# Float32 tiles for U and the scores in an attention and gated feed-forward kernel

## The chip, the cores and the metric

The kernel runs on one core of a Trainium2 chip. The metric is the time of one execution on the device in microseconds (us), the median of the runs; lower is better. A core has TensorE (matrix products, results in PSUM; its weight loads have a row of their own, PEld), VectorE (DVE), ScalarE (ACT), GpSimd (POOL) and SyncE (SP), which here issues the DMA transfers. Each engine works through its own list of instructions in order.

## The reference

Eight batches, eight heads, 576 tokens, head width 64, 32 memory slots; the model width is 512, the hidden width 1536. The first part compresses each head's keys and values into 32 slots, the second is a gated feed-forward layer on all 4608 tokens:

```
a    = softmax over tokens of phi                  # [b, h, 576, 32]
k_m  = a.T k ;  v_m = a.T v                        # [b, h, 32, 64]
attn = softmax over slots of (q k_m.T / 8)         # [b, h, 576, 32]
x    = attn v_m, heads side by side                # [b * 576, 512]
out  = (sigmoid(x w_gate) * (x w_val)) w_out       # float32
```

Everything but the weights is float32; the three weight matrices arrive as float64.

## The kernel before, in words

The host only rearranges the inputs. The kernel never makes x. It uses x w = attn (v_m w): for a batch and 128 hidden columns (an *f tile*, 12 of them) it makes U = v_m [w_gate | w_val] with one row for each head and slot (8 x 32 = 256 rows, as two groups of 128) and 256 columns, and multiplies the softmax by it. Products that need more than TensorE's fast float32r gives are made as three: each operand is split into a rounded part (`hi`, by ScalarE) and what rounding left (`lo`, a subtraction), and hi hi + lo hi + hi lo are summed in PSUM.

**Memory of a batch** (`memory`): phi's softmax over tokens (`a_max`, `a_exp`), transposed by TensorE (L292, L296), times k and v (L312: float32 products of 32 columns, one for each head of a group, beside one another in TensorE). VectorE scales the result and masks it so that two heads stand block-diagonal; TensorE transposes it (L330).

**Scores and softmax** (`scores`, `s_exp`, `attend`): for each 128 tokens four float32 products, q stationary (128x128) and the block-diagonal k_m moving (64 columns, L367), so tokens lie on the partitions and the softmax over slots is a reduction along the row. Ten transposes by TensorE (L414) then turn the result to [(head, slot), token] in `at_hi` and `at_lo`.

**U** (`make_u`): v_m of two batches (a *pair*) as hi and lo, block-diagonal over both, is the stationary operand; w as hi and lo is moving. For each f tile twelve products of 256 columns (L465 to L467) give U for both batches of the pair. One batch's U is used soon; the other's is parked in SBUF as float32 (`u_par`) and split later (`unpark`). `split_w` splits w anew for every pair: float32 w is kept in DRAM (`w32`), stored once and loaded again for each pair.

**A step** is one batch and one f tile. `gate_half` is called for 256 and for 320 tokens: twelve products (L508), a sigmoid on ScalarE, the multiplication on VectorE (L518), the split of the result (L519, L528). `out_half` multiplies by w_out (L543 to L545) three half steps later (`LAG = 3`). The last 64 tokens of a batch are gathered for `out_left` (L575 to L577).

**Order.** The first pair takes its 24 steps in turns of four f tiles (`CHUNKS`), so that the weights can be converted meanwhile; the other pairs take twelve f tiles of one batch, then twelve of the other. Beside the steps, generators (`sides`) are advanced a piece at a time: the scores, softmax and memory of the batches to come. `convert_w` and `convert_wo` turn float64 words to float32, 512 columns at a time (`to_f32`: one operation on ScalarE, four on VectorE, L132 to L141); `due` spreads them over the first pair. At the very start `queued` fixes the order of the pieces by hand. The scheduler of the framework then places instructions on the engines by its own estimate, so traced order and built order differ. Loads leave SP in the traced order (`load`).

Of the kernel before, what the change touches and what calls it, by code (L numbers as in the profile page):

```python
# [25 lines left out]
CUT = [slice(0, 2 * P), slice(2 * P, S)]   # tokens of one gate / value product  # L26
SCALE = 1.0 / 8.0
# [8 lines left out]
SOLO = 1          # f tiles whose U is made before the second batch's memory is known  # L36
CHUNKS = [4, 4, 4]   # f tiles of the first two batches between their turns
# [3 lines left out]
def attn_moe_kernel(  # L41
    ctx: ExitStack,
    tc: tile.TileContext,
    qT: bass.AP,      # [B, 128 (head of pair, d), 4 * S]   token pieces of (4 pairs, tokens)
    kvm: bass.AP,     # [B, 2, 128, 4, 512]   s = c * 128 + p ; (head, k | v)
    kvt: bass.AP,     # [B, 128, 512]         (group, s - 512)
    phiT: bass.AP,    # [B, 128 (head, m), 2, S]   the second group's last 64 tokens first
    wgv: bass.AP,     # [12, 128, 4, 256]     (gate 128 | value 128), float64 as words
    wo: bass.AP,      # [12, 128, DM]         float64 as words
    out: bass.AP,     # [B * S, DM]  # L50
# [4 lines left out]
    wp = ctx.enter_context(tc.tile_pool(name="wp", bufs=1))  # L55
# [7 lines left out]
    # the accumulators' banks serve too until there is something to accumulate  # L63
# [9 lines left out]
    def att(shape, name, bufs):  # L73
        return sb.tile(shape, F32, name=name, bufs=bufs)
# [3 lines left out]
    # mask[row, j, :] = 1 where the row's head is of parity j  # L78
    mask = keep.tile([P, 2, D], F32, name="mask")
    nc.vector.memset(mask, 0.0)  # L80
    for h in range(4):
        nc.vector.memset(mask[h * M : (h + 1) * M, h % 2, :], 1.0)
# [196 lines left out]
    def memory(b):  # L279
# [55 lines left out]
        if b == 0:  # L335
            nc.scalar.copy(*kmT)
# [561 lines left out]
```

## Time and profile before

| | us |
|---|---|
| runs (3) | 823.63, 824.36, 825.55 |
| median | 824.36 |
| span of the profiled execution | 823.0 |
| TensorE busy in it | 782.0 (95%) |
| VectorE busy | 496.8 (60%) |
| ScalarE busy | 433.1 (53%) |
| GpSimd busy | 195.4 (24%) |

The span runs from the first to the last instruction of one profiled execution. In the views below a row of TensorE's timeline has start, length, line, operation, output <- inputs, tile, shape and count; the ends of products are modelled and overlap, so what one product costs in a stream is read from the distance of two starts, not from its length. A float32 product stands as two records. "L508" is line 508 of the kernel before.

### The profile page before, as it was taken

How to read it: one execution, taken by the hardware profiler on the slowest of the kernel's cores; microseconds unless marked ns; L12 is line 12 of the kernel's file. 1: busy time of each engine (PE TensorE's matmuls, PEld its weight loads, DVE VectorE, ACT ScalarE, POOL GpSimd, SP SyncE). 2: the span in 40 equal slices, each digit the busy share in tenths (PEclk: the TensorE clock that was granted, in tenths of full speed). 3: DMA queues.
4: the chain of work that ended last, by engine and by line, in shares of the span. 5: the costliest groups of instructions: out<-in, count | busy, mean ns of one | idle time of the engine just before them, and what ended most of it. 6: DMA issues, size and time to landing. Idle time of an engine off the chain costs nothing.

```text
span 823.0 us, 13982 instructions
## 1 busy us (share of the span) xinstructions
PE 782.0 (95%) x5394; PEld 699.7 (85%) x5394; DVE 496.8 (60%) x1000; ACT 433.1 (53%) x940; POOL 195.4 (24%) x128
## 2 busy tenths in 40 slices
PE   6887889899899999999999999999999999999997
PEld 5775877788799879998899889999889899999996
DVE  3799997999755564565454464556553654454432
ACT  3557766565534485645325377554424576653222
POOL 1245533435612142311002133220101232310000
PEclk8889999999999999999999999999999999999999
DMA  9857646774732312412030421604000312101001
GB/s 357 327 180 260 246 149 216 256 256 138 241 106 78 134 52 106 167 52 84 30 142 26 160 64 52 219 29 135 1 2 26 104 39 78 53 1 52 1 1 65
DMA packets 30227, 96.33 MB, mean 117 GB/s; under 512 B 3408, under 2 KB 4432, under 8 KB 28112
## 3 DMA queue, kind: packets, MB, share of 16 engines
q1 hardware_dynamic: 30160, 95.43, 33.2%
q8 instruction: 42, 0.69, 0.4%
q14 instruction: 25, 0.20, 0.1%
HBM read 75.50 MB, written 19.92 MB: 116 GB/s over the span
## 4 chain that ended last, share of the span: by engine, by line
PE 73%; DVE 8%; ACT 3%; DMA 3%; issue 2%; SPq 0%; DVEq 0%; ACTq 0%
PE pu_t L508 30%; PE acc L545 9%; PE acc L543 9%; PE acc L544 9%; DMA words<-in_wo_dram 3%; PE pu_t L367 2%; PE pu_t L465 2%; PE pu_t L466 2%; PE pu_t L467 2%; PE pu_t L577 1%; PE pu_t L576 1%; DVE bits L138 1%; PE pu_t L575 1%; DVE g_lo L528 1%; PE pu_t L312 1%
## 5 line engine op out<-in xcount | busy, mean ns | idle before, releaser
L508 PE MATMUL pu_t<-at_hi,u_hi 128*128 128x256 f32 (+1 forms) x768 | 233.5, 304 | 12.4 <-DVE prod L518 6.2
L508 PE MATMUL pu_t<-at_lo,u_hi 128*128 128x256 f32 (+1 forms) x768 | 227.1, 296 | 0.0
L508 PE MATMUL pu_t<-at_hi,u_lo 128*128 128x256 f32 (+1 forms) x768 | 226.6, 296 | 0.2 <-DVE u_lo L116 0.2
L116 POOL TENSOR_TENSOR w_lo<-wraw,w_hi 128x1024 fp32r<-128x1024 f32 (+1 forms) x50 | 117.8, 2356 | 358.1 <-ACT w_hi L204 358.1
L508 PEld LDWEIGHTS pu_t<-at_hi,u_hi 128*128 128x128 f32 x768 | 145.8, 190 | 25.2 <-DVE prod L518 8.6
L518 DVE TENSOR_TENSOR prod<-pu_t,sg 128x256 f32<-128x256 f32 x192 | 87.2, 454 | 128.4 <-ACT sg L103 88.1
L543 PE MATMUL acc<-wo_hi,g_hi 128*128 128x512 f32 x384 | 153.6, 403 | 4.7 <-ACT g_hi L519 2.5
L103 ACT ACTIVATE sg<-pu_t 128x256 f32<-128x256 f32 x192 | 78.4, 410 | 147.0 <-PE pu_t L508 145.8
L544 PE MATMUL acc<-wo_lo,g_hi 128*128 128x512 f32 x384 | 152.0, 396 | 0.0
L508 PEld LDWEIGHTS pu_t<-at_lo,u_hi 128*128 128x128 f32 x768 | 145.8, 190 | 6.5
L545 PE MATMUL acc<-wo_hi,g_lo 128*128 128x512 f32 x384 | 142.9, 399 | 5.3 <-DVE g_lo L528 5.3
L508 PEld LDWEIGHTS pu_t<-at_hi,u_lo 128*128 128x128 f32 x768 | 145.6, 190 | 1.6 <-DVE u_lo L116 0.9
L519 ACT CAST g_hi<-prod 128x256 fp32r<-128x256 f32 x192 | 77.7, 405 | 114.9 <-DVE prod L518 113.3
L528 DVE TENSOR_TENSOR g_lo<-prod,g_hi 128x256 fp32r<-128x256 f32 x168 | 81.6, 486 | 39.0 <-ACT g_hi L519 38.8
L545 PEld LDWEIGHTS acc<-wo_hi,g_lo 128*128 128x128 f32 x384 | 70.9, 189 | 21.2 <-DVE g_lo L528 6.9
L543 PEld LDWEIGHTS acc<-wo_hi,g_hi 128*128 128x128 f32 x384 | 72.5, 189 | 17.5 <-ACT g_hi L519 4.3
L544 PEld LDWEIGHTS acc<-wo_lo,g_hi 128*128 128x128 f32 x384 | 72.6, 189 | 10.2 <-POOL wo_lo L116 0.3
L116 DVE TENSOR_TENSOR u_lo<-pu_t,u_hi 64x512 fp32r<-64x512 f32 x82 | 56.4, 688 | 34.1 <-ACT u_hi L474 32.9
L471 ACT COPY u_par<-pu_t 64x512 f32<-64x512 f32 x110 | 63.4, 579 | 11.1 <-DVE u_lo L116 9.3
L465 PE MATMUL pu_t<-w_hi,vm_hi 128*128 128x256 f32 x196 | 55.2, 286 | 4.1 <-ACT w_hi L204 3.8
L204 ACT CAST w_hi<-wraw 128x1024 fp32r<-128x1024 f32 (+1 forms) x51 | 51.8, 1016 | 13.3 <-DVE wraw L141 13.0
L466 PE MATMUL pu_t<-w_hi,vm_lo 128*128 128x256 f32 x196 | 54.6, 283 | 0.0
(102 smaller groups left out, 1024.1 us busy)
## 6 DMA issues: line engine op xcount, KB each, us to landing
wraw<-w SPq DMA_DIRECT2D x37, 512.0 KB, 3.4
kvm<-in_kvm_dram SPq DMA_DIRECT2D x16, 1024.0 KB, 8.1
words<-in_wgv_dram SPq DMA_DIRECT2D x24, 512.0 KB, 5.2
qt<-in_qT_dram SPq DMA_DIRECT2D x16, 512.0 KB, 6.5
out_dram<-row SPq DMA_DIRECT2D x32, 256.0 KB, 2.4
words<-in_wo_dram SPq DMA_DIRECT2D x12, 512.0 KB, 4.8
w<-wraw SPq DMA_DIRECT2D x12, 512.0 KB, 3.0
ph<-in_phiT_dram SPq DMA_DIRECT2D x8, 576.0 KB, 4.9
```

Source lines behind the costliest of these rows:

```text
L103: last_act[0] = nc.scalar.activation(*args, **kw)
L116: engine.tensor_tensor(lo, x, hi.bitcast(F32), op=ALU.subtract)
L465: nc.tensor.matmul(pb[:, g, :], l_hi, whi[:, kt, :], start=True, stop=False)
L466: nc.tensor.matmul(pb[:, g, :], l_lo, whi[:, kt, :], start=False, stop=False)
L471: nc.scalar.copy(par[j][rs], pb[rs])
L508: nc.tensor.matmul(pt[:, :n], l[:, g, ws], r[:, g, cs], start=(i == 0), stop=(i == 5))
L518: nc.vector.tensor_tensor(prod[:, :n], ps[1][:, :n], sg[:, :n], op=ALU.mult)
L519: nc.scalar.copy(ghi, prod[:, : 2 * P])
L528: nc.vector.tensor_tensor(glo, prod[:, : 2 * P], ghi.bitcast(F32), op=ALU.subtract)
L543: nc.tensor.matmul(o, hi[:, ts], w_hi, start=at_start, stop=False)
L544: nc.tensor.matmul(o, hi[:, ts], w_lo, start=False, stop=False)
L545: nc.tensor.matmul(o, lo[:, ts], w_hi, start=False, stop=at_end)
```

## The change

What it does:

- U is made for one batch at a time. v_m stays float32 and is not split or laid out block-diagonal for two batches: `make_u` multiplies 64x32 of it, one head, by 64 rows of w (which hold that head's part of the model width), for two f tiles at once (512 columns; one f tile for the first four of batch 0). Eight such products, one for each head, fill two PSUM banks. The results are [(head, slot), columns] as before. ScalarE rounds whole banks to `u_hi`, VectorE subtracts for `u_lo`; nothing is parked.
- w_gate | w_val as float32 stays in SBUF for all twelve f tiles (`wg`). Its copy in DRAM, its loads and its splitting are gone.
- The scores are made the other way round: 64x32 of k_m is stationary and q is moving (256 tokens, then 320 as 256 + 64), so heads and slots lie on the partitions. VectorE transposes 32x32 blocks out of PSUM, so that slots lie along the row; after the softmax it transposes back. TensorE's ten transposes for each batch are gone.
- `memory` writes k_m and v_m in float32 without mask.
- In the conversion the limit to float32's range (L132) goes from VectorE to GpSimd.
- Buffers: words 4 (then 2) for 7 (then 3), rows 2 for 3; w_out's first 9 f tiles have room from the start for 8. The table `CONVERT` says at which step each f tile is converted. The first loads leave as phi, k and v, q's first 256 tokens, two pieces of w, the rest of q, the second batch's phi, two pieces of w, the second batch's k and v.
- The remainders of the gates go to GpSimd for batches 0 and 1 (before: batch 0).

The diff, cut:

```diff
-LAG = 3           # half steps between a gate and its product with w_out
-NE = 8            # f tiles of w_out for which there is room from the start
-GAP = 2           # steps from one f tile's U to the next, at least, where there is time
-BITS, ROW, WORDS = 2, 3, (7, 3)   # buffers
+LAG = 3
+NE = 9
+ALONE = 4
+CONVERT = [0, 1, 3, 4, 6, 7, 9, 11, 13, 15, 16]
+WORDS, BITS = (4, 2), (2, 1)
...
+    wg = keep.tile([P, NFT, NKT, 256], F32, name="wg")
...
-    w32 = [dram.tile([P, NKT, 256], F32, name=f"w32_{i}") for i in range(NFT)]
...
+    def to_bits(f, k):
...
         nc.scalar.activation(bits.bitcast(F32), words[:, :, 1].bitcast(F32), AF.Abs)
+        nc.gpsimd.tensor_scalar(
+            bits.bitcast(F32), bits.bitcast(F32), HUGE, TINY, op0=ALU.min, op1=ALU.max
+        )
...
-        nc.vector.tensor_scalar(
-            bits.bitcast(F32), bits.bitcast(F32), TINY, HUGE, op0=ALU.max, op1=ALU.min
-        )
...
+    def of_head(b, w, p):
+
+        rs = slice((p % 2) * D, (p % 2 + 1) * D)
+        hs = slice((p % 4) * M, (p % 4 + 1) * M)
+        return rs, kvTs[b][w][rs, p // 4, hs]
+
+    def scores(b, c):
+
+        n = CUT[c].stop - CUT[c].start
+        nb = n // 32
+        pb = [bank(), bank()]
+        o = 0
+        for u, nu in PIECES[c]:
+            qt = loaded.pop((b, "q", u))
+            for p in range(H):
+                rs, l = of_head(b, 0, p)
+                js = slice((p // 2) * M, (p // 2 + 1) * M)
+                nc.tensor.matmul(
+                    pb[p % 2][js, o : o + nu], l, qt[rs, p // 2, :], start=True, stop=True
+                )
+            o += nu
...
+        for r in range(2):
+            nc.vector.transpose(
+                e[:, r * nb : (r + 1) * nb, :].rearrange("p w m -> p (w m)"), pb[r][:, :n]
+            )
+        mx = att([P, 2 * nb], "mx")
+        nc.vector.tensor_reduce(mx, e, axis=AX.X, op=ALU.max)
+        nc.vector.tensor_tensor(
+            e, e, mx.unsqueeze(2).broadcast_to([P, 2 * nb, M]), op=ALU.subtract
+        )
...
+    def turn(b, c):
...
+        for r in range(2):
+            nc.vector.transpose(
+                t[:, r, :n], e[:, r * n // M : (r + 1) * n // M, :].rearrange("p w m -> p (w m)")
+            )
+        nc.scalar.copy(hi[:, :, cs], t[:, :, :n])
+        rest(lo[:, :, cs], t[:, :, :n], hi[:, :, cs])
...
+    def make_u(b, fs):
+
+        nf = len(fs)
+        pb = [bank()[:, : nf * 256].rearrange("p (f x) -> p f x", f=nf) for _ in range(2)]
+        for p in range(H):
+            rs, l = of_head(b, 1, p)
+            js = slice((p // 2) * M, (p // 2 + 1) * M)
+            r = wg[rs, fs[0] : fs[0] + nf, ORDER[b % 2][p] // 2, :]
+            nc.tensor.matmul(pb[p % 2][js], l, r, start=True, stop=True)
...
+        for r in range(2):
+            nc.scalar.copy(hi[:, r, :nf], pb[r])
+            rest(lo[:, r, :nf], pb[r], hi[:, r, :nf])
...
+    for i, (b, f, at_start, at_end) in enumerate(steps):
...
+        gate_half(b, f, 1)
+        if i + 1 < len(steps) and steps[i + 1][0] != b:
+            run(beside)
+        if i in u_at:
+            make_u(*u_at[i])
...
+        while len(pend) >= LAG:
+            out_half(*pend.pop(0))
```

TensorE's built order in the second or third pair, where a U stands. Before (u, at: U and the softmax; w, vm: w and v_m; pu_t: a PSUM bank):

```order
L508 MATMUL pu_t<-at_hi,u_lo 128x256
L465 MATMUL pu_t<-w_hi,vm_hi 128x256
L466 MATMUL pu_t<-w_hi,vm_lo 128x256
L467 MATMUL pu_t<-w_lo,vm_hi 128x256
L465 MATMUL pu_t<-w_hi,vm_hi 128x256
L466 MATMUL pu_t<-w_hi,vm_lo 128x256
L467 MATMUL pu_t<-w_lo,vm_hi 128x256
```

The same place with the change (wg: the kept w; vT: v_m; acc: the accumulators of the output; L417 to L419 are the products with w_out, L387 those of the gate):

```order
L387 MATMUL pu_t<-at_hi,u_lo 128x320
L356 MATMUL pu_t<-wg,vT 32x512 x4
L417 MATMUL acc_3853<-wo_hi,g_hi 128x512
L418 MATMUL acc_3853<-wo_lo,g_hi 128x512
L419 MATMUL acc_3853<-wo_hi,g_lo 128x512
L417 MATMUL acc_3857<-wo_hi,g_hi 128x512
L418 MATMUL acc_3857<-wo_lo,g_hi 128x512
L356 MATMUL pu_t<-wg,vT 32x512 x4
L419 MATMUL acc_3857<-wo_hi,g_lo 128x512
```

Twelve products in a row have become eight in two runs of four, with products of the output between them; the first run has the four heads with rows 0 to 63, the second those with rows 64 to 127.

VectorE's built order in the third step of the first pair, with the change (sg: the gate's sigmoid and product; bits, words: a piece of float64 weights under conversion; wg and row: its result):

```order
L397 TENSOR_TENSOR sg_616<-pu_t_603,sg_616 128x256
L150 TENSOR_SCALAR bits_493<-bits_493 128x512
L153 SCALAR_TENSOR_TENSOR bits_493<-words_392,bits_493 128x512
L156 SCALAR_TENSOR_TENSOR wg_82<-words_392,bits_493 128x512
L150 TENSOR_SCALAR bits_502<-bits_502 128x512
L153 SCALAR_TENSOR_TENSOR bits_502<-words_400,bits_502 128x512
L156 SCALAR_TENSOR_TENSOR row_501<-words_400,bits_502 128x512
L397 TENSOR_TENSOR sg_657<-pu_t_650,sg_657 128x320
```

Between the two multiplications of one step stand two whole pieces of conversion, three operations each where there were four. Ahead of the first step's multiplication VectorE's order has 2 pieces (before: 3), ahead of the ninth step's 28 (before: 23), ahead of the seventeenth's 36, all of them (before: 32).

More of the change, by code (lines that the diff above doesn't have):

```diff
@@ L271, in a_exp @@
         loaded[b, "rz"] = rz
-    def new_vm(pair):
-        if pair not in vm:
-            vm[pair] = [
-                keep.tile([P, NKT, 2, D], F32R, name=n, bufs=2) for n in ("vm_hi", "vm_lo")
-            ]
     def memory(b):
@@ L477, in unpark @@
-    def unpark(b, f):
-        if (b, f) in U:
-            return
-        par = parked.pop((b, f))
-        hi = mb.tile([P, NG, 256], F32R, name="u_hi", bufs=2)
-        lo = mb.tile([P, NG, 256], F32R, name="u_lo", bufs=2)
-        nc.vector.tensor_copy(hi, par)
-        rest(lo, par, hi, nc.gpsimd if b == 0 else nc.vector)
-        U[b, f] = (hi, lo)
+        kvTs[b] = [keep.tile([P, NG, P], F32, name=f"{w}T", bufs=2 + (w == "v")) for w in "kv"]
+        for w in range(2):
+            nc.scalar.copy(kvTs[b][w], kvT[:, w])
@@ L615, in piece, with step @@
                 next(g, None)
+    def step(do, *args, **kw):
+        with queued():
+            return do(*args, **kw)
     def warm(n):
@@ L648, in attn_moe_kernel @@
[L648 to L659 removed]
+    steps = [s for pair in range(B // 2) for s in turns(pair)]
@@ L660, in attn_moe_kernel @@
+    u_at = {}
+    for i, (b, f, _, _) in enumerate(steps):
+        if b == 0 and f < ALONE:
+            u_at[i - 1] = (b, [f])
+        elif f % 2 == 0:
+            u_at[i - 1] = (b, [f, f + 1])
+    spare = ident.bitcast(mybir.dt.bfloat16)
     idle = po.tile([P, 512], F32, name=f"acc{SF - 1}")
-    once = att([P, NG], "z", 1)[:, :1]
-    with queued():
-        curve(once, mask[:, 0, :1], AF.Exp)
+    once = att([P, NG], "z")[:, :1]
+    step(curve, once, ident[:, :1], AF.Exp)
     load_phi(0)
@@ L681, in attn_moe_kernel @@
-    m0, s0, m1, a0 = memory(0), scores(0), memory(1), attend(0)
-    bits = {}
-    def prepare(f, k):
-        bits[f, k] = to_bits(words_of[f, k])
-    def convert(f, k):
-        both = [None, None]
-        both[k] = bits.pop((f, k))
-        convert_w(f, (k,), both)
-    def step(do, *args, **kw):
-        with queued():
-            do(*args, **kw)
-    def expo(u):
-        s_exp(0, SP_U[u : u + 1])
+    m0, m1 = memory(0), memory(1)
+    bits = {}
     warm(16)
@@ L739, in score @@
     def score(b, then=None):
-        yield from scores(b)
+        for c in range(2):
+            scores(b, c)
+            yield
         if then is not None:
@@ L744, in score @@
             yield
-            yield
-        s_exp(b)
+        for c in range(2):
+            s_exp(b, c)
         if then is not None:
@@ L749, in score, with attend @@
         if b + 1 < B:
-            load_q(b + 1)
+            for c in range(2):
+                load_q(b + 1, c)
         yield
+    def attend(b):
+        for c in range(2):
+            normalize(b, c)
+        yield
+        for c in range(2):
+            turn(b, c)
+            yield
     def remember(b, ready=False):
+        if b >= B:
+            return
         if not ready:
@@ L766, in load_next, with then @@
             load_kv(b)
[L768 to L780 removed]
+    def then(b):
+        return b if b < B else None
+    sides = {0: [m1, score(1), attend(1)]}
```

504 lines of the change are left out of this document (139 added, 365 removed).

## The prediction

> **What bounds the kernel now.** I read the busy times by stretch first. The cuts are the first gate product (38.5 us), the ninth step (129.1), the first step of the second pair of batches (255.7), of the third and fourth pair, the last product of the last gate step (805.8).
>
> ```profile
> core 0: us, PE busy (x) PEld busy (x) DVE busy (x) ACT busy (x) POOL busy (x), PEclk, DMA share, GB/s
> 0.00:38.50 38.50, 29.14 (x306) 24.10 (x306) 22.27 (x55) 16.81 (x35) 6.66 (x15) 0.87 0.91 355
> 38.50:129.10 90.60, 74.75 (x498) 63.73 (x497) 86.71 (x153) 58.58 (x114) 39.94 (x27) 0.92 0.59 211
> 129.10:255.70 126.60, 118.24 (x806) 104.69 (x805) 98.75 (x181) 70.77 (x154) 52.55 (x38) 1.00 0.56 188
> 255.70:445.60 189.90, 188.50 (x1331) 170.80 (x1331) 103.73 (x219) 98.59 (x218) 34.87 (x18) 1.00 0.27 92
> 445.60:635.50 189.90, 188.50 (x1331) 170.79 (x1330) 99.71 (x215) 99.68 (x220) 34.48 (x18) 1.00 0.22 75
> 635.50:805.80 170.30, 170.30 (x1076) 155.65 (x1075) 80.84 (x171) 85.25 (x192) 26.87 (x13) 1.00 0.13 40
> 805.80:823.00 17.20, 12.56 (x55) 9.92 (x53) 4.79 (x10) 3.37 (x8) 0.00 (x0) 0.94 0.23 77
> ```
>
> From 255.7 us to 805.8 TensorE is never idle for long, and VectorE, ScalarE and the DMA engines are half idle: only what TensorE itself has to do counts there. From 38.5 to 129.1 VectorE is busy 86.71 of 90.60 us: it sets the pace. Between 129.1 and 255.7 both are near their limits. The chain of waits gives the price of a step, by the starts of the same products one step apart (start, length, what).
>
> ```profile
> 448.65 1.73 PE pu_t L367 x16
> ...
> 533.46 1.42 PE pu_t L508 x12
> 540.85 1.42 PE pu_t L508 x12
> ...
> 638.55 1.73 PE pu_t L367 x16
> ...
> 790.96 1.76 PE pu_t L508 x12
> 796.89 1.76 PE pu_t L508 x12
> ```
>
> A pair takes 638.55 - 448.65 = 189.90 us. A step that makes a U takes 540.85 - 533.46 = 7.39, one without 796.89 - 790.96 = 5.93, so the twelve products of one U cost 1.46 us of TensorE, whole.
>
> **U, part by part.** Removed are twelve full-array products for each f tile of a pair: 1.46 us. Added are eight float32 products, 64 rows by 32 columns, of 512 columns, for each batch and two f tiles: again one group for each f tile of a pair. The trace has no 64x32 product. The nearest are the 32-column float32 products of the memory (L312), here in TensorE's timeline between full-array products.
>
> ```profile
> 325.40 0.31 PE L508 MATMUL pu_t<-at_lo,u_hi 128*128 128x320 f32 x1
> 325.55 0.31 PE L508 MATMUL pu_t<-at_hi,u_lo 128*128 128x320 f32 x1
> 325.79 1.08 PE L312 MATMUL pu_t<-kvm,e 128*32 128x128 f32 x32
> 326.69 0.40 PE L312 MATMUL pu_t<-kvt,tails 128*32 128x128 f32 x8
> 326.90 1.06 PE L312 MATMUL pu_t<-kvm,e 128*32 128x128 f32 x32
> 327.78 0.40 PE L312 MATMUL pu_t<-kvt,tails 128*32 128x128 f32 x8
> 328.11 0.39 PE L508 MATMUL pu_t<-at_hi,u_hi 128*128 128x256 f32 x1
> 328.33 0.28 PE L508 MATMUL pu_t<-at_lo,u_hi 128*128 128x256 f32 x1
> 328.45 0.28 PE L508 MATMUL pu_t<-at_hi,u_lo 128*128 128x256 f32 x1
> ```
>
> The program has 40 of these products, the trace 80 records: a float32 product is two records. 80 records, 20 for each of four column tiles, need 0.110 us for each four (326.90 - 325.79 = 1.11 for 40). So four tiles side by side cost what one would, 0.110 us for one record of 128 columns. Going in and out costs more: before the run products start 0.15 apart, so one would have started at 325.70; behind it they start 0.12 apart, and the second one starts at 328.33. The run has taken 328.33 - 0.12 - 325.70 = 2.51 us, 20 x 0.110 of them its records: 0.31 us are lost for each run of small tiles between full-array products.
>
> How many runs there are is in TensorE's new order, shown with the change. The scheduler has put the eight in two runs of four, first the heads whose rows are 0 to 63, then the others, with full-array products between: the two halves of the rows never work together. 33 of the 35 groups between 255.7 and 805.8 are cut like this, the other two 1 + 7.
>
> A run of four is two records side by side, of 512 columns each. Upper bound, in proportion to columns: 2 x 4 x 0.110 = 0.88. Lower bound: nothing of 512 columns goes by faster than the 0.23 of these rows, so 2 x 0.23 = 0.46.
>
> ```profile
> 502.68 0.60 PE L292 MATMUL pu_t<-ident,ph 128*128 128x128 f32 x4
> 503.04 0.48 PE L543 MATMUL acc<-wo_hi,g_hi 128*128 128x512 f32 x1
> 503.36 0.39 PE L544 MATMUL acc<-wo_lo,g_hi 128*128 128x512 f32 x1
> 503.59 0.39 PE L543 MATMUL acc<-wo_hi,g_hi 128*128 128x512 f32 x1
> ```
>
> I take 0.86, near the proportional end, because L312 has the same type and tile width. A group in two runs is then 2 x (0.86 + 0.31) = 2.34 us (1.54 at the lower bound), and I count one in 1 + 7 the same. For 35 groups: 35 x 2.34 = 81.9 against 35 x 1.46 = 51.1, **+30.8 us** (+2.8 at the lower bound).
>
> Weighed against the skill: the row leaves open whether a record's 0.110 us is streaming or a fixed cost. The Trainium skill, "FP8 and Floating Point Precision", section "TensorE Precision Notes", gives true float32 four passes through the array, two for each of the two records; estimated from that page, streaming grows with the columns, and by it the term is the +30.8 and not the +2.8. No run here has shown it yet.
>
> **Scores and turns.** The old scores of one 256-token half and the 64-token rest:
>
> ```profile
> 363.92 0.40 PE L545 MATMUL acc<-wo_hi,g_lo 128*128 128x512 f32 x1
> 364.15 1.89 PE L367 MATMUL pu_t<-kmT,qt 128*128 128x64 f32 x16
> 365.85 0.39 PE L508 MATMUL pu_t<-at_hi,u_hi 128*128 128x320 f32 x1
> ...
> 26.04 0.68 PE L367 MATMUL pu_t<-kmT,qt 128*64 128x64 f32 x8
> 26.65 0.66 PE L292 MATMUL pu_t<-ident,ph 128*128 128x128 f32 x4
> ```
>
> 365.85 - 364.15 = 1.70 twice, 26.65 - 26.04 = 0.61 once, some 0.08 for each change: 4.2 us a batch. The new ones are 64x32 tiles of 256 columns; in the built order the first half stands in three or four runs, the rest in one of 16 (twice four of 256 columns, twice four of 64: 0.44 + 0.44 + 0.11 + 0.11): by the same rule 3 x (0.44 + 0.31) + 1.1 + 0.31 = 3.7 us. Five batches fall between 255.7 and 805.8: -2.5. The ten transposes of the softmax leave TensorE; four cost 503.04 - 502.68 = 0.36 plus 0.09 by which the product behind is late, so two fours and a two some 1.1 a batch: -5.5. VectorE takes them as eight extra operations a batch, some 0.45 each by its other 256- and 320-column operations, 3.6 us where it is idle half of the time: nothing (3.6 a batch if it were not). The stretch from 255.7 gets 30.8 - 8 = **+22.8 us**.
>
> **Before 255.7.** VectorE's conversions from float64, rows of VectorE's groups up to 129.1 us:
>
> ```profile
> L138 DVE SCALAR_TENSOR_TENSOR bits<-words,bits 128x512 int32<-128x512 int32 x22 | 22.7, 1032 | 0.3
> L132 DVE TENSOR_SCALAR bits<-bits 128x512 f32<-128x512 f32 x23 | 16.0, 694 | 0.3 <-ACT bits L122 0.3
> L135 DVE TENSOR_SCALAR bits<-bits 128x512 int32<-128x512 int32 x23 | 12.2, 531 | 0.3
> L141 DVE SCALAR_TENSOR_TENSOR wraw<-words,bits 128x512 int32<-128x512 int32 x15 | 10.7, 712 | 0.1
> ```
>
> A quarter (512 columns of float64 words, one call of the conversion) costs 1.03 + 0.69 + 0.53 + 0.71 = 2.97 us. L132 moves to GpSimd: 2.27. But the new order converts earlier: on VectorE, ahead of the first gate's multiplication stood 3 quarters and now 2, ahead of the ninth step's 23 and now 28. In its new order, shown with the change, they stand two and three together between the gates' multiplications. So in the first eight steps 26 x 2.27 = 59.0 us of conversions stand where 20 x 2.97 = 59.4 did. Of the other 86.7 - 59.4 = 27.3, U's remainders get some 4 cheaper, the second batch's softmax and the row copies some 8 dearer: about 92 us of VectorE for eight steps, 96 with the idle share of before. They begin earlier: the second half of k and v lands at 10.26 and the first gate starts at 38.52 now.
>
> ```profile
> 10.26 1.08 PE L312 MATMUL pu_t<-kvm,left 128*32 128x128 f32 x32 [1.11 <-DMA kvm<-in_kvm_dram]
> 38.52 0.38 PE L508 MATMUL pu_t<-at_hi,u_hi 128*128 128x256 f32 x1
> ```
>
> With q's first piece queued next, half the scores and no split of w, I count some 20 us of operations in a row behind 10.26: 30 us (bounds 25 and 38.5). The ninth step then starts at 126 instead of 129.1. From there to the second pair TensorE has sixteen steps of 5.93, eight groups of 2.34, two memories (each the 2.5 of L312 and 13 transposes, some 4) and the scores of a batch: 94.9 + 18.7 + 8 + 3.7 = 125.3, with a few us of waits 129, instead of 126.6. Together **-1 us** (-11 to +12). Four conversion buffers for words instead of seven, and two rows instead of three where tiles are kept between turns, lie behind 40 us of conversions in hand and the next turn's first products: nothing, up to 8 us if not. The loads and stores of w that go moved, after 255.7, on engines that are 0.27 busy: nothing.
>
> **Sum.** 823.0 + 22.8 - 1 = 844.8 in the profiled execution's span. The runs before took 823.63 to 825.55, their median 824.36, so 1.4 us lie around the span: **846 us**, 2.6% more than the median.
>
> **The rivals.** (1) *Float32 tiles stream faster than in proportion*: the lower bound of 0.46. Then U costs +2.8, the scores of a batch 2.6 instead of 3.7 (0.23 for each 0.44), so -10.7 after 255.7, and the eight groups and the scores ahead of it 7.4 less than before: 824.4 - 18 = 806. The change turns faster where a run of four streams for less than 0.6 us, a group for less than 1.83 with its changes of tile. For it: the 0.110 might be a fixed cost. Against: float32 would then pass 512 columns as fast as the type that needs one record where it needs two.
>
> (2) *All eight at once*: a group is 0.86 + 0.31 = 1.17, so U -10 instead of +30.8 and 9 less ahead: 796. It needs the second four to start while the first four stream, as in the five groups that stand as eight in a row or that alternate. The Trainium skill, "TensorEngine Tiling (Array Packing)", section "Available Configurations", lists 64x32 as eight independent tiles. Against it: full-array products between the runs in 33 of 35 groups, which need the rows of both.
>
> (3) *U comes late.* Its copy and remainder start behind the second run, and the gate that reads them follows some nine products later, 9 x 0.23 = 2.1 us.
>
> ```profile
> L474 ACT CAST u_hi<-pu_t 64x512 fp32r<-64x512 f32 x82 | 47.6, 581 | 9.7 <-PE pu_t L467 8.6
> L116 DVE TENSOR_TENSOR u_lo<-pu_t,u_hi 64x512 fp32r<-64x512 f32 x82 | 56.4, 688 | 34.1 <-ACT u_hi L474 32.9
> ```
>
> A copy of 0.58 and two remainders of 0.69 are 1.96: just hidden. With a us of other work ahead of them on ScalarE or VectorE, 35 us come on top: 881.
>
> (4) *The four tiles do not overlap* where they have 64 rows: 4 x 0.88 + 0.31 a run, 43 groups x 2 x 2.7 more: 1075. The same four column tiles overlap in L312.
>
> **Chances.** Forecast 0.62, (1) 0.12, (2) 0.05, (3) 0.13, (4) 0.03, gains before 255.7 that just cancel the rest 0.05. The forecast's own range, with the two ends before 255.7 and a run of 0.75 to 0.9, is 832 to 860; 8 times in 10 it should be 814 to 866, into (1) and the near side of (3). Faster by over 0.2% 0.17, within 0.2% (what the spread of the runs can tell) 0.05, slower 0.78.
>
> **What would show it.** Groups of L356 four and four, some 0.43 us between the two records of a tile, 0.3 around a run; steps of 5.93 unchanged and a pair of some 197 us instead of 189.9; VectorE over 90% busy until about 126 us. The forecast is wrong if a run of four ends in half a us, if the pair is shorter than 190, or if the second pair starts before 240.

## The result, and the profile after

The changed kernel takes **842.85 us** (median of 4 runs, 842.42 to 843.12), the kernel before 824.0 (4 runs, 822.14 to 825.55): a ratio of **1.0227, 95% interval 1.021 to 1.0244**. It is slower, by 19 us. The profiled execution has a span of 840.5 us against 823.0.

The busy times by stretch of the changed kernel come first, cut where the prediction cut the kernel before: first gate product, ninth step, the second, third and fourth pair of batches, last gate product. (The prediction's last cut, 805.8 us, lies 1.2 us behind the end of the last gate product before, at 804.6.)

```profile
core 0: us, PE busy (x) PEld busy (x) DVE busy (x) ACT busy (x) POOL busy (x), PEclk, DMA share, GB/s
0.00:28.40 28.40, 14.95 (x189) 9.77 (x189) 13.50 (x28) 8.83 (x19) 2.94 (x9) 0.86 0.94 369
28.40:132.60 104.20, 81.67 (x617) 61.66 (x618) 86.18 (x146) 57.05 (x119) 46.69 (x52) 0.83 0.58 204
132.60:255.90 123.30, 121.26 (x849) 93.96 (x848) 66.45 (x119) 52.15 (x127) 39.82 (x48) 1.00 0.39 128
255.90:448.40 192.50, 192.07 (x1369) 147.84 (x1368) 87.49 (x185) 74.47 (x184) 4.89 (x4) 1.00 0.17 59
448.40:643.80 195.40, 194.97 (x1374) 149.52 (x1373) 85.47 (x182) 75.62 (x186) 4.89 (x4) 1.00 0.12 40
643.80:822.00 178.20, 177.66 (x1110) 138.70 (x1109) 71.23 (x147) 62.32 (x156) 2.77 (x2) 1.00 0.04 14
822.00:840.50 18.50, 13.77 (x60) 10.90 (x59) 5.54 (x11) 3.97 (x10) 0.00 (x0) 0.98 0.22 71
```

The second pair starts at 255.9 us as it did at 255.7 before, and the tail behind the last gate product takes 18.4 us before (from 804.6) and 18.5 after. All the loss lies between, where TensorE is never idle: the middle pair takes 195.4 us instead of 189.9. Two kinds of waits of TensorE are all that the list of waits from 255 to 822 us holds:

```profile
PE pu_t L387 <- ACT sg L98: 0.9, 2, 0.4
PE acc L417 <- ACT g_hi L398: 0.5, 1, 0.5
```

So it is TensorE's own work that grew. TensorE's timeline (start, length, what; an x of 8 is eight records, two for each float32 product) shows a U of one group at the end of the program, and three other places with small tiles:

```profile
251.99 1.09 PE L356 MATMUL pu_t<-wg,vT 64*32 64x512 f32 x16
253.00 0.50 PE L417 MATMUL acc<-wo_hi,g_hi 128*128 128x512 f32 x1
...
260.65 0.80 PE L297 MATMUL pu_t<-qt,kT 64*32 64x256 f32 x32
261.38 0.39 PE L387 MATMUL pu_t<-at_hi,u_hi 128*128 128x256 f32 x1
...
268.95 1.04 PE L356 MATMUL pu_t<-wg,vT 64*32 64x512 f32 x2
269.92 0.50 PE L449 MATMUL pu_t<-wo_hi,g_lo 128*128 128x512 f32 x1
...
778.96 1.06 PE L356 MATMUL pu_t<-wg,vT 64*32 64x512 f32 x8
779.95 0.50 PE L417 MATMUL acc<-wo_hi,g_hi 128*128 128x512 f32 x1
780.38 1.06 PE L356 MATMUL pu_t<-wg,vT 64*32 64x512 f32 x8
781.37 0.50 PE L418 MATMUL acc<-wo_lo,g_hi 128*128 128x512 f32 x1
781.71 0.39 PE L419 MATMUL acc<-wo_hi,g_lo 128*128 128x512 f32 x1
```

At 778.96 and 780.38 stand the two runs of four, with one full-array product between. From the start of a run to the next product pass 0.99 us. The price of the whole group is in the chain of waits, by the same twelve gate products two steps apart:

```profile
791.58 1.76 PE pu_t L387 x12
...
805.90 1.76 PE pu_t L387 x12
```

805.90 - 791.58 = 14.32 us for two steps that share one group; two steps without a U took 2 x 5.92 before, so a group costs 14.32 - 11.84 = **2.48 us**, where the old twelve products cost 1.46.

The other three places say more. At 251.99 all eight products happen to stand in a row: 16 records, and the next product starts after 1.01 us. At 268.95 one product stands alone, two records, 0.97 us. One tile, four tiles or eight tiles take the same time. And the run of the scores at 260.65, eight products of 256 columns and eight of 64, takes 0.73 us.

Where the 17.4 us went, from the start of each TensorE product to the start of the next, summed over the second pair's first gate product to the last (255.7 to 804.6 us before, 255.9 to 822.0 after; the last column is the first experiment, 246.4 to 775.8):

```
                                     before   after   eight together
U (and the claims of its banks)        50.4    69.5    42.1
gates                                 232.2   238.5   235.7
w_out, with the last 64 tokens        228.1   232.3   228.6
scores                                 20.1    11.9     9.3
transposes of the softmax               4.9     0       0
memory and its transposes              13.2    14.0    14.1
sum                                   548.8   566.2   529.7
```

U's own products take 19.1 us more, and the full-array products another 10.5: the second one behind a run starts 0.34 us after the first (781.37, 781.71 above) and not 0.23. How much of the 10.5 stands there the table doesn't tell. Scores and transposes give 13 back.

### The profile page after: what moved, and what is told of

It reads as the page before. It is cut to its first block, busy times and chain, and to the rows that moved or that the text cites. A ratio compares the mean times of both kernels' runs of the same rounds, so it can differ in the third digit from the quotient of the medians.

```text
span 840.5 us, 13734 instructions
## 1 busy us (share of the span) xinstructions
PE 796.3 (95%) x5560; PEld 612.3 (73%) x5560; DVE 415.9 (49%) x813; ACT 334.4 (40%) x799; POOL 102.0 (12%) x118
## 4 chain that ended last, share of the span: by engine, by line
PE 83%; DVE 8%; DMA 3%; ACT 3%; issue 2%; POOL 1%; SPq 0%; ACTq 0%; DVEq 0%; POOLq 0%
PE pu_t L387 33%; PE acc L417 10%; PE pu_t L356 10%; PE acc L418 10%; PE acc L419 10%; PE pu_t L260 2%; DVE bits L153 2%; PE pu_t L297 2%; PE pu_t L449 1%; PE pu_t L448 1%; PE pu_t L447 1%; DMA ph<-in_phiT_dram 1%; DMA part<-row 1%; DMA row<-part 1%; PE pu_t L240 1%
## 5 line engine op out<-in xcount | busy, mean ns | idle before, releaser
L387 PE MATMUL pu_t<-at_hi,u_hi 128*128 128x256 f32 (+1 forms) x768 | 230.6, 306 | 19.0 <-ACT at_hi L342 12.2
L387 PE MATMUL pu_t<-at_lo,u_hi 128*128 128x256 f32 (+1 forms) x768 | 228.7, 300 | 0.4 <-DVE at_lo L111 0.4
L387 PE MATMUL pu_t<-at_hi,u_lo 128*128 128x256 f32 (+1 forms) x768 | 223.7, 300 | 0.4 <-DVE u_lo L111 0.4
L397 DVE TENSOR_TENSOR sg<-pu_t,sg 128x256 f32<-128x256 f32 x192 | 86.1, 454 | 219.4 <-ACT sg L98 176.5
L387 PEld LDWEIGHTS pu_t<-at_hi,u_hi 128*128 128x128 f32 x768 | 147.5, 192 | 35.1 <-ACT at_hi L342 13.4
L417 PE MATMUL acc<-wo_hi,g_hi 128*128 128x512 f32 x384 | 156.3, 412 | 3.4 <-ACT wo_hi L175 2.7
L387 PEld LDWEIGHTS pu_t<-at_lo,u_hi 128*128 128x128 f32 x768 | 148.0, 193 | 6.5 <-DVE at_lo L111 1.0
L387 PEld LDWEIGHTS pu_t<-at_hi,u_lo 128*128 128x128 f32 x768 | 145.9, 192 | 5.8 <-issue 1.6
L419 PE MATMUL acc<-wo_hi,g_lo 128*128 128x512 f32 x384 | 148.1, 401 | 0.0
L417 PEld LDWEIGHTS acc<-wo_hi,g_hi 128*128 128x128 f32 x384 | 72.0, 189 | 55.1 <-issue 29.3
L398 ACT CAST g_hi<-sg 128x256 fp32r<-128x256 f32 x192 | 77.5, 405 | 83.8 <-DVE sg L397 79.0
L356 PE MATMUL pu_t<-wg,vT 64*32 64x512 f32 (+1 forms) x800 | 100.7, 589 | 8.5 <-DVE wg L156 8.0
L111 DVE TENSOR_TENSOR u_lo<-pu_t,u_hi 128x512 fp32r<-128x512 f32 (+1 forms) x100 | 66.2, 665 | 72.0 <-ACT u_hi L361 72.0
L419 PEld LDWEIGHTS acc<-wo_hi,g_lo 128*128 128x128 f32 x384 | 71.7, 189 | 25.1 <-issue 12.1
L361 ACT CAST u_hi<-pu_t 128x512 fp32r<-128x512 f32 (+1 forms) x100 | 55.6, 566 | 63.1 <-PE pu_t L356 63.0
L111 DVE TENSOR_TENSOR g_lo<-sg,g_hi 128x256 fp32r<-128x256 f32 x144 | 60.8, 423 | 37.0 <-ACT g_hi L398 33.9
L327 POOL TENSOR_TENSOR e<-e,zs 128x512 f32<-128x512 f32 (+1 forms) x16 | 20.3, 1266 | 421.9 <-DVE zs L326 401.0
L111 POOL TENSOR_TENSOR g_lo<-sg,g_hi 128x256 fp32r<-128x256 f32 x48 | 39.6, 832 | 64.0 <-ACT g_hi L398 49.2
L356 PEld LDWEIGHTS pu_t<-wg,vT 64*32 64x32 f32 x800 | 15.3, 105 | 34.0 <-issue 17.6
```

What stands on the lines that cost most here:

```text
L111: engine.tensor_tensor(lo, x, hi.bitcast(F32), op=ALU.subtract)
L327: engine.tensor_tensor(e, e, zs.unsqueeze(2).broadcast_to([P, n, M]), op=ALU.mult)
L356: nc.tensor.matmul(pb[p % 2][js], l, r, start=True, stop=True)
L361: nc.scalar.copy(hi[:, r, :nf], pb[r])
L387: nc.tensor.matmul(pt[:, :n], l[:, g, ws], r[:, g, cs], start=(i == 0), stop=(i == 5))
L397: nc.vector.tensor_tensor(prod[:, :n], ps[1][:, :n], sg[:, :n], op=ALU.mult)
```

## The experiments

All times are medians, and ratios go against the kernel before on the same chip. The starts come from the profiled executions, by the gates' first products.

```
                     us      ratio (95%)              first gate  ninth step  second pair   span
before             824.0                                 38.5       129.1       255.7      823.0
after              842.85  1.0227 (1.0210 to 1.0244)     28.4       132.6       255.9      840.5
eight together     795.73  0.9662 (0.9630 to 0.9695)     28.1       131.7       246.4      794.4
one pass           794.11  0.9640 (0.9595 to 0.9684)     30.0       133.2       256.0      791.6
filled             839.63  1.0191 (1.0160 to 1.0221)     35.0       133.1       254.8      839.7
clamp back         844.84  1.0254 (1.0226 to 1.0282)     28.8       137.5       258.4      843.5
three rows         843.78  1.0250 (1.0228 to 1.0272)     29.4       133.3       255.2      842.2
no shift           837.11  1.0168 (1.0148 to 1.0189)     27.5       128.8       250.3      835.6
memory later       838.54  1.0187 (1.0170 to 1.0204)     29.0       125.4       252.3      837.0
scores together    792.40  0.9626 (0.9605 to 0.9646)     28.7       132.2       246.6      791.0
all, three rows    793.10  0.9651 (0.9615 to 0.9688)     28.1       130.1       246.0      789.6
all, memory later  792.42  0.9626 (0.9606 to 0.9647)     28.4       122.0       245.5      789.7
```

### The eight products in one piece

My theory was that U's price is the two runs, and that the row halves, once neighbours, share one. The rivals were that the halves follow each other even then, and that U comes late.

```diff
+    def touch(banks):
+        tiny = ident.bitcast(mybir.dt.bfloat16)
...
+                last = nc.tensor.matmul(o[:, :64], tiny[:, :P], tiny[:, :64], start=True, stop=True)
+        return last
...
+        both = touch(pb)
         for p in range(H):
...
-            nc.tensor.matmul(pb[p % 2][js], l, r, start=True, stop=True)
+            with tc.issue_after(both.ins), tc.high_priority():
+                nc.tensor.matmul(pb[p % 2][js], l, r, start=True, stop=True)
```

> The changed kernel, with the eight products of each U kept in one piece: two very small products (64 columns) first claim both PSUM banks, and then all eight follow with nothing between, the two row halves in turn. In the changed kernel a group comes in two runs of four, 1.23 to 1.42 us from the product before a run to the product behind it, so that two steps with one group take 14.32 us against 2 x 5.92 without: 2.48 us a group. Theory A, the row halves can work together: the run of eight takes the time of one run of four, as the one at 251.99 us does that happens to stand so (1.09 us long, 1.02 to the next product). Then some 1.24 us a group go and 0.1 for the two small products come: 35 groups x 1.14 = 40 us behind the second pair's start and a few us ahead of it, 797 to 805 us in all, pairs of 182 us instead of 195.4. Theory B, the halves follow each other: a run of eight takes about 2 us, only one change of tile (some 0.25) is saved a group, and 835 to 842 us result. Theory C, U becomes late because both halves are copied out at the same end: the products are short as in A, but gates wait on the copies, and 820 to 843 us result.

Measured: 795.73 us. All 46 groups of 512 columns stand in one run. TensorE's timeline of this kernel, and its two middle pairs by stretch:

```profile
751.94 0.20 PE L357 MATMUL pu_t<-ident 128*128 128x64 bf16 x1
752.07 1.09 PE L370 MATMUL pu_t<-wg,vT 64*32 64x512 f32 x16
753.09 0.50 PE L431 MATMUL acc<-wo_hi,g_hi 128*128 128x512 f32 x1
753.43 0.39 PE L432 MATMUL acc<-wo_lo,g_hi 128*128 128x512 f32 x1
```

```profile
246.40:429.20 182.80, 181.45 (x1400) 148.80 (x1399) 86.24 (x185) 73.32 (x185) 5.02 (x4) 1.00 0.18 62
429.20:611.20 182.00, 181.13 (x1400) 148.86 (x1399) 84.13 (x181) 73.89 (x186) 5.02 (x4) 1.00 0.13 43
```

Eight tiles take 1.02 us where four took 0.99, and the pair falls from 195.4 to 182.0. Theory A holds, with a whole time just under its range; B and C fall (TensorE's waits from 246 to 776 us are 2.5 us in all). The Trainium skill, "TensorEngine Tiling (Array Packing)", section "Key Properties", says that tiles load and multiply independently, and that a change of tiling mode drains TensorE; the rows agree with both: eight for the time of one, and the next two full-array products start 1.02 and 0.34 us on where full-array products are 0.23 apart. The price of a group, again from two steps that share one, is in this kernel's chain of waits:

```profile
756.15 6.36 PE pu_t L401 x48
...
769.48 6.36 PE pu_t L401 x48
```

13.33 - 11.84 = 1.49 us, about the 1.46 of the old twelve products. So the loss of the change was not in the small tiles, but in the full-array products that the scheduler had put between their halves. Why it put them there is not shown. That the second bank came free later is one explanation; but the edit claims both banks, ties the eight products behind the claim and gives them priority, all at once, and these were not tried apart.

### One pass instead of float32

```diff
             r = wg[rs, fs[0] : fs[0] + nf, ORDER[b % 2][p] // 2, :]
+            if b >= 2:
+                tiny = ident.bitcast(mybir.dt.bfloat16)
+                l, r = tiny[rs, :M], tiny[rs].unsqueeze(1).broadcast_to([D, nf, 2 * P])
```

> The changed kernel, with U's products of the batches from the third on made of bf16 ones and zeros (the identity) in place of w and v_m: same tiles of 64x32, same 512 columns, same order; the values of U are left out. It tells what in the run of four is the type. Forecast's step: a float32 product is two records of which each needs more than one pass over the columns; a bf16 product is one record that goes by at the 0.23 us per 512 columns of the full-array products. Then a run of four ends after some 0.35 us instead of 1.06, a group costs 2 x (0.23 + 0.3) = 1.06 instead of 2.48, and 35 groups x 1.4 = 50 us go: 788 to 798 us. Rival, the run's cost is the tiles and not the type (each product has its weights to load, a run its two changes of tile): a run stays at 0.8 us or more and the whole above 825 us.

Measured: 794.11 us. TensorE's timeline, a run of four:

```profile
759.79 0.31 PE L390 MATMUL pu_t<-at_hi,u_lo 128*128 128x320 f32 x1
760.03 0.40 PE L359 MATMUL pu_t<-ident 64*32 64x512 bf16 x4
760.35 0.50 PE L420 MATMUL acc<-wo_hi,g_hi 128*128 128x512 f32 x1
```

Same tiles, same columns, and 0.33 us from the run to the next product (760.03 and 760.35 are rounded) instead of 0.99. How often float32 passes over its columns follows with a third run, of 256 float32 columns in the changed kernel:

```profile
256.19 0.64 PE L297 MATMUL pu_t<-qt,kT 64*32 64x256 f32 x8
256.76 0.39 PE L387 MATMUL pu_t<-at_hi,u_lo 128*128 128x256 f32 x1
```

It takes 0.57 us: 256 columns less save 0.42. So 512 columns of float32 are some 0.84 of the 0.99 us, and 0.15 is left that doesn't grow with the columns. If that is the same for bf16, 0.33 - 0.15 = 0.18 is one pass over 512 columns; a full-array product of 512 takes 0.23. 0.84 is 4.7 times the one and 3.7 times the other, so about four passes. Four is what the Trainium skill gives true float32 ("FP8 and Floating Point Precision", "TensorE Precision Notes"), and the runs agree as far as they go. The rival, that the price is the tiles and not the type, falls.

### The eight steps before 132.6 us

The total fitted the forecast, but the ninth step came at 132.6 us and not at 126. Five runs looked for what holds it. First the granted clock, which the prediction had not looked at. The changed kernel by 10 us:

```profile
20.00:30.00 10.00, 2.67 (x15) 1.79 (x16) 7.26 (x14) 2.05 (x5) 1.40 (x2) 0.52 1.02 413
30.00:40.00 10.00, 5.04 (x20) 4.29 (x20) 5.51 (x12) 6.11 (x12) 3.19 (x4) 0.50 0.08 30
...
90.00:100.00 10.00, 5.58 (x24) 5.28 (x25) 9.90 (x15) 4.96 (x8) 6.19 (x6) 0.50 0.56 163
100.00:110.00 10.00, 7.97 (x44) 6.05 (x44) 5.17 (x12) 7.92 (x15) 1.89 (x2) 0.88 0.78 258
```

PEclk, the third number from the right, falls to 0.50 to 0.52 in the first three of these windows, where TensorE is busy 2.7 to 5.6 us of 10. The edit fills such places with small products:

```diff
+IDLE = {(0, 0, 0): 64, (0, 0, 1): 48, (0, 1, 0): 32, (1, 0, 0): 72, (1, 0, 1): 48}
...
+            if w == 0:
+                tiny = ident.bitcast(mybir.dt.bfloat16)
+                for _ in range(IDLE.get((b, f, c), 0)):
+                    nc.tensor.matmul(pt[:, :256], tiny[:, :P], tiny, start=True, stop=True)
             ws = slice(w * P, (w + 1) * P)
```

> The changed kernel, with 264 small bf16 products (256 columns, into a bank that the real product overwrites) put ahead of five gate halves where TensorE stood idle before 100 us. It tests why the eight steps behind the first gate took 104.2 us (28.4 to 132.6) and not 96. Theory of the clock: the granted clock was 0.50 to 0.67 at 20 to 50 us and 0.50 to 0.77 at 80 to 100 us, where TensorE was busy a quarter to a half, and the gate products there took 3.9 us a half instead of 1.9 to 2.0; with TensorE kept busy the clock stays near 1.00, the ninth step starts at 122 to 128 us, and the whole takes 834 to 840 us. Rival, the round trips between VectorE, ScalarE and GpSimd set the pace: the clock rises too, but the ninth step stays within 2 us of 132.6 and the whole within 2 of 842.9. Rival 2: the added products stand in the way, since they are queued ahead of the real ones: 264 x 0.11 to 0.2 is up to 40 us, and what does not fit into the idle time comes on top, 845 to 860 us.

Measured: 839.63 us, within the range of the clock theory; but its interval overlaps that of the changed kernel. The same windows of this kernel:

```profile
30.00:40.00 10.00, 10.00 (x93) 9.14 (x92) 4.78 (x11) 5.03 (x9) 2.50 (x3) 1.00 0.09 36
...
90.00:100.00 10.00, 10.00 (x75) 8.71 (x73) 9.54 (x17) 6.11 (x10) 6.39 (x6) 1.00 0.50 154
```

The clock is back at 1.00 in these windows, and the ninth step starts at 133.1: there the theory of the clock falls. Between the fourth step and the ninth the clock of the changed kernel was 0.77 and 0.50 in the windows from 80 to 100 us. The stretch takes 61.8 us in it (70.8 to 132.6) and 62.8 with the filling (70.3 to 133.1), so the slow products there cost nothing that can be seen. Ahead of the fourth step the run changed two things: the first gate came 6.6 us later, at 35.0, and the clock was higher, and at the fourth step nothing is left of the delay. Whether the first gate was off the path or the clock bought the delay back, this run alone can't tell. The kernel of the one-pass run, the same as the changed one up to there, has its first gate 1.6 us later and its fourth step only 0.4, so the path has at least some room there.

The second candidate is VectorE, from both sides: the clamp given back to it, and one of its operations left out.

```diff
-        nc.gpsimd.tensor_scalar(
+        nc.vector.tensor_scalar(
             bits.bitcast(F32), bits.bitcast(F32), HUGE, TINY, op0=ALU.min, op1=ALU.max
```

> The changed kernel, with the clamp of each quarter's conversion back on VectorE (0.69 us each in the kernel before) instead of GpSimd (0.75 us here). 26 quarters fall into the 104.2 us from the first gate to the ninth step, in which VectorE is busy 86.2 us. Account of the prediction, VectorE sets the pace there: 26 x 0.69 = 18 us more of VectorE, the ninth step at 143 to 150 us instead of 132.6, the whole 848 to 860 us. Rival, the 18 us in which VectorE is idle take them up, because waits between the engines and not VectorE's work set the pace: the ninth step moves by less than 4 us and the whole by less than 3. Rival 2, the trip to GpSimd and back costs more than the work it saves: the ninth step comes earlier, the whole takes 836 to 842 us.

Measured: 844.84 us, the ninth step at 137.5. VectorE's groups of the changed kernel from 28.4 to 132.6 us, then of this one from 28.8 to 137.5:

```profile
L153 DVE SCALAR_TENSOR_TENSOR bits<-words,bits 128x512 int32<-128x512 int32 x25 | 22.3, 892 | 0.6
L156 DVE SCALAR_TENSOR_TENSOR wg<-words,bits 128x512 int32<-128x512 int32 x17 | 15.0, 884 | 0.3
L150 DVE TENSOR_SCALAR bits<-bits 128x512 int32<-128x512 int32 x25 | 12.9, 514 | 1.0 <-POOL bits L138 1.0
L156 DVE SCALAR_TENSOR_TENSOR row<-words,bits 128x512 int32<-128x512 int32 x7 | 6.3, 906 | 1.6 <-DMA part<-row 1.4
```

```profile
L153 DVE SCALAR_TENSOR_TENSOR bits<-words,bits 128x512 int32<-128x512 int32 x25 | 20.8, 832 | 0.2
L156 DVE SCALAR_TENSOR_TENSOR wg<-words,bits 128x512 int32<-128x512 int32 x17 | 15.2, 893 | 0.2
L138 DVE TENSOR_SCALAR bits<-bits 128x512 f32<-128x512 f32 x25 | 12.9, 516 | 0.0
L150 DVE TENSOR_SCALAR bits<-bits 128x512 int32<-128x512 int32 x25 | 11.7, 469 | 0.2
L156 DVE SCALAR_TENSOR_TENSOR row<-words,bits 128x512 int32<-128x512 int32 x7 | 5.3, 752 | 0.1
```

The clamp is 12.9 us and not 18, and the other four groups become 3.5 us shorter together (1.5 + 1.2 + 1.0 - 0.2) with the clamp gone from GpSimd. Records of neighbours overlap, so the groups add up to more than the busy time: that is 93.0 us in this stretch against 86.2, only 6.9 more. The ninth step moves by 4.9, the second pair by 2.5, and in the whole time no difference can be told (the intervals overlap). None of the three theories of the expectation had the ninth step right; what the run shows is that most of VectorE's added work counts up to the ninth step.

```diff
-        nc.vector.tensor_scalar(
-            bits, bits, 3, 0x3FFFFFFF, op0=ALU.logical_shift_left, op1=ALU.bitwise_and
-        )
```

> The changed kernel without the first of the three VectorE operations of each conversion (the shift and mask, 0.51 us each in the stretch from the first gate to the ninth step, 25 of them: 12.9 us); the weights are then other numbers. The counterpart to the run that put 18 us more on VectorE and moved the ninth step by 4.9 us. Theory, VectorE's work sets the pace in the part where it is over 98% busy (60 to 100 us, about ten conversions, 5 us) and nothing else does: the ninth step at 126 to 129 us instead of 132.6, the second pair 2 to 4 us earlier, the whole 838 to 841 us. Rival, VectorE paces all of the eight steps: 13 us earlier, 119 to 121 us, the whole 829 to 833 us. Rival 2, other waits end there anyway: less than 2 us, the whole 841 to 844 us.

Measured: 837.11 us, the ninth step at 128.8, 3.8 us earlier, and the second pair 5.5 earlier. VectorE is busy 76.4 us of the eight steps instead of 86.2, 9.8 less, so here less than half of the difference counts. The ninth step is as the first theory had it, the second pair and the whole a little better. VectorE paces a part of the eight steps. The theory put this part at 60 to 100 us, where the 10 us windows show VectorE full (9.90 of 10 at 90 us, but 5.17 at 100). The marks inside don't settle it: with the clamp back, the loss arises behind the fourth step (70.4 us against 70.8 there, 120.1 against 113.3 at the seventh), but without the shift 3.2 us are won by the fourth step already (67.6), and still 3.2 at the sixth (96.8 against 100.0). What stands in the way behind 100 us is in the chain of waits of the changed kernel:

```profile
102.70 0.59 ACT row L426
103.29 0.34 ACT sg L98
103.65 1.28 ACT L98
104.94 1.63 ACT ph L98 x4
106.59 1.28 ACT L98
```

ScalarE copies a row, does one sigmoid, and then the exponentials of the third batch's phi between two table loads of 1.28 us; the next gate's sigmoid comes behind them, and VectorE waits 1.53 us for it.

```diff
-    sides[c0] = [remember(2)]
+    sides[c0 + CHUNKS[0]] = [remember(2)]
```

> The changed kernel with the memory of the third batch (its maxima, exponentials with two table loads, 13 transposes and 80 product records) begun at the ninth step instead of the fifth. In the changed kernel VectorE is busy only 5.2 of 10 us from 100 to 110 us, when ScalarE does these exponentials and TensorE stands idle 2 us, and TensorE is busy without a gap from 110 to 130. Theory, from 110 us on TensorE's work sets the end: the ninth step comes some 5 to 8 us earlier (4 us of TensorE, 2 of idle time), but the work comes back behind it: second pair within 2 us of 255.9, the whole 841 to 844 us. Rival, ScalarE's exponentials and table loads hold the gates up at the fifth step and are hidden later: second pair 2 to 5 us earlier, the whole 837 to 841 us. Rival 2, the memory comes too late for the third batch's scores: the second pair starts behind 258 us, 845 us or more.

Measured: 838.54 us (ratio 1.0187, 1.017 to 1.0204, just below the interval of the changed kernel). The ninth step comes 7.2 us earlier, and of that 3.6 are left at the second pair, 4 in the whole time. The numbers are those of the first rival: begun at the fifth step, the third batch's memory holds up the gates; begun at the ninth, half of that disappears. My theory that all of it comes back falls. The run moved the whole memory, TensorE's 4 us of it too, so that ScalarE's exponentials are the part that holds the gates is argued from the chain and not shown.

The prediction had also put two rows instead of three at nothing. The edit here is `bufs=3` for `row`, and one buffer for words in the last part of the conversions instead of two, to make room.

> The changed kernel, with three buffers for the rows of w_out and of the partial results instead of two, as the kernel before had them; so that it fits, the last part of the conversions has one buffer for words instead of two. The prediction counted the two rows at nothing, up to 8 us if not. In the changed kernel VectorE waits 6.2 us in four places between 30 and 260 us for a row that is still being stored, and the chain of waits up to the ninth step holds such a store for 4.88 us. Theory, this wait is on the path: the ninth step starts 3 to 8 us before 132.6, the whole takes 836 to 841 us. Rival, something else ends at nearly the same time: less than 2 us from 132.6, the whole 841 to 845 us. Rival 2, the one buffer for words makes the last conversions late: the ninth step comes earlier, but the second pair starts behind 257 us, 845 us or more.

Measured: 843.78 us, the ninth step at 133.3. VectorE's waits for a row that is being stored fall from 6.2 us to 0.7 between 30 and 260 us, and nothing is gained. The first rival holds. The four buffers for words instead of seven were not tried.

### The faster version

The scores of a half get the same claim of their two banks, on top of the eight products in one piece.

```diff
         pb = [bank(), bank()]
+        both = touch(pb)
...
-                nc.tensor.matmul(
+                with tc.issue_after(both.ins), tc.high_priority():
+                    nc.tensor.matmul(
```

> The kernel whose U is made by eight products in one piece, with the scores treated likewise: two small products claim the banks, then the 8 or 16 products of a half follow with nothing between. The first half of a batch's scores stood in two runs of four there; one run of four of 256 columns was 0.62 us long in the changed kernel and cost 0.8 us with its changes of tile, and a small product costs 0.086. Theory, the row halves work together here too: 0.8 - 4 x 0.086 = 0.45 us less a batch, 3 to 4 us in all, 791.5 to 793.5 us. Rival, the claims cost what the run saves, since TensorE holds two banks longer and gates wait for one: 795 to 800 us.

Measured: 792.40 us, a ratio of **0.9626 (0.9605 to 0.9646)** to the kernel before: 30 us faster than it, 50 faster than the changed kernel. Its two middle pairs:

```profile
246.60:428.20 181.60, 180.34 (x1407) 148.96 (x1406) 85.06 (x185) 73.23 (x185) 5.03 (x4) 1.00 0.19 63
428.20:609.00 180.80, 180.02 (x1408) 149.06 (x1407) 82.97 (x181) 74.08 (x186) 5.03 (x4) 1.00 0.13 44
```

The pair loses another 1.2 us and the medians differ by 3.3, as the theory had it, though the intervals of the two kernels overlap. Two more were added to it, the three rows and the later memory.

> U and scores each in one piece, and three rows with one late buffer for words. If the two other runs' theories hold, their gains add up: 786 to 791 us. If rows do nothing, it is the time of the kernel with U and scores in one piece, within 1.5 us.

> U and scores each in one piece, and the memory of the third batch begun at the ninth step. Theory, the two gains lie in different stretches and add up: 792.4 - 4.3 = 788 us, between 786 and 790. Rival, the gates of the first eight steps were held up by the divided runs too, so that part of the gain is in the 792.4 already: 791 to 793 us.

Measured: 793.10 and 792.42 us. Neither adds anything that can be told, though with the later memory the ninth step comes at 122.0 us, 10 earlier: the second pair starts only 1.1 us earlier. Both miss the ranges of their theories (786 to 791 and 786 to 790). The rival of the second had its time right, 791 to 793, but not its reason: undivided runs alone had brought the ninth step only from 132.6 to 132.2. Why the 4 us of the later memory do not carry over is not settled; the stretch from the ninth step to the second pair takes 123.6 us in that kernel, 119.5 of them busy on TensorE, against 114.4 without the later memory, so most of what was moved out of the eight steps is paid there.

## Why the prediction was right, and where it was not

The forecast was 846 us; 842.85 came. By its steps:

- **What bounds the kernel.** Right. From 255.9 to 822 us TensorE waits 1.4 us in all, and the loss lies there: +17.4 us, where +22.8 was forecast.
- **U.** Right in mechanism: two runs of four for nearly every group, each paid in full, no overlap of the row halves. "2 x (0.86 + 0.31) = 2.34 us" measured 2.48, a run 0.99 with the changes of tile on top. The forecast was +30.8 us over 35 groups; by the price of a group in the last pair it is 35 x 1.02 = +35.7, by the table of starts 19.1 for U's own products and up to 10.5 for those behind them. The choice between 0.46 and 0.86 for a run decided the sign. The prediction took 0.86 because L312 has the same type and tile width, and the one-pass run bears this out: it is the type.
- **Scores and turns.** Right in sign, the scores mis-sized: "3.7 us" a batch measured 11.9 / 5 = 2.4, so five batches gave -8.2 us and not -2.5. The step that failed is the run of sixteen, counted as "0.44 + 0.44 + 0.11 + 0.11" and 0.31 around it, with its row halves one after the other; they alternate in the built order and run together, 0.73 us at 260.65. The prediction had used for neighbours the price that holds for parted halves. The other runs, counted at 0.44 + 0.31 = 0.75 each, take some 0.57 to the next product. The transposes, -5.5 forecast, were -4.9, and 0.8 went to the memory's own.
- **Before 255.7 us.** "-1 us" measured +0.1, but that is luck: two errors cancel. The first gate came at 28.4 (30 forecast). The eight steps then took 104.2 us and not 96: the failed step is "about 92 us of VectorE for eight steps, 96 with the idle share of before". Its own terms, 59.0 + 27.3 - 4 + 8, add up to 90.3 and not to 92. The busy time was less still, 86.2, but VectorE was idle for 18.0 us, 17% where it had been 4%; the sign named for this step, over 90% busy, did not come. VectorE is full from 60 to 100 us, and behind that the third batch's memory stands in the way (begun later, it gives 7.2 us back). The sum also counted from the first gate on, but when the first gate came 6.6 us later in the filled run, at a higher clock, the ninth step stayed. Against it, from the ninth step to the second pair, 129 forecast and 123.3 measured: two of the eight groups there stand whole, the scores are cheaper, and the "few us of waits" did not come.
- **Buffers.** "Nothing" held for the rows. The words' buffers were not tried.
- **The rivals.** (1), tiles that stream faster: a run of 0.99 excludes it. (2), all eight at once: the groups were parted, so the time of 796 did not come, but its mechanism is true wherever the eight are neighbours, and the experiment that makes them so takes 795.73. The prediction had the condition right; that the number fits so well is luck, since a whole group costs 1.49 us and not 1.17, while the five batches' scores give back 10.8 us (20.1 to 9.3) and not 2.5. (3), U late: 1.4 us of waits in 566. (4), no overlap of four: a run of four takes what one product takes (0.99 and 0.97 us).

## What to carry to other kernels

Count small-tile work by runs between full-array products, not by products: here one, four or eight 64x32 float32 products cost the same microsecond of TensorE, and what parts a run doubles the price. So look at the built order before the arithmetic, and where a scheduler parts tiles that write to different banks, let something cheap claim the banks first and keep the group behind it in one piece. And a total that fits can hide two wrong steps; compare the marks inside it, too.

## What the runs showed of the hardware

- A run of 512 float32 columns is about as long with one tile (0.97 us to the next product) as with eight (1.01), in both directions of the array: the four column tiles and the two row halves, which write to different banks here.
- The granted clock is 0.50 to 0.52 in three windows of 10 us where TensorE is busy 2.7 to 5.6, and 1.00 in the two of them that small products fill to 10. Here that made no difference to the whole time that can be told.
- Some of VectorE's operations were shorter with less on GpSimd beside them: with the clamp moved off GpSimd, the same last step of a conversion to a row fell from 906 to 752 ns, the middle one from 892 to 832. Both read two SBUF inputs, and the Trainium skill, "GPSIMD Engine Reference", section "Specifications", names contention with GpSimd over the SBUF interfaces for such instructions and for those in a 2-port perf mode. But the shift, with one input, fell too (514 to 469; no run shows its mode), and the last step into w did not (884 and 893), so no run here isolates it.
